# Weights that arrive as 64-bit floats: pieces of 256 columns, a first stage in plain floats, and sign words by two multiplications on GpSimd

## The chip, the core and the metric

One core of one Trainium2 chip runs the kernel. Times are device microseconds of one execution, and fewer is better. The core has five engines, which run side by side: PE (TensorE, the matmuls; its weight loads are listed as PEld), DVE (VectorE), ACT (ScalarE), POOL (GpSimd) and SP, which here only issues DMAs. They wait for each other by semaphores.

## What is computed

```
p_packed = attention(p, k, v)                 # p is [8, 8, 32, 64]; k, v are [8, 8, 576, 64]
out      = attention(q, p_packed, p_packed)   # q is [8, 8, 576, 64]
x = out, heads side by side                   # [4608, 512]
h = x @ w_in                                  # w_in is [512, 2048], float64
g = h * tanh(softplus(h))                     # Mish
result = g @ w_out                            # w_out is [2048, 512], float64; result float32
```

## The kernel before

**The fold.** Since x is the second attention's probabilities times p_packed, the kernel multiplies p_packed into w_in first. For each of the 8 batches it makes a packed weight (`wp`, from `weave`: matmuls `ps_w<-wi,ppT`, ppT being p_packed transposed). Attention then gives only the transposed probabilities `aT`, in two halves g = 0, 1 of 128 rows (4 heads × 32) by 576 tokens. A batch is done in 16 groups, one for each 128 columns of w_in; I count groups as t = 16 b + f.

**A group.** `up(hf)` multiplies the packed weight of 128 columns by `aT` for 288 of the 576 tokens. Each product is made of three matmuls in a faster float format, of values that are split in a high and a low part: `wp_hi, wp_lo` (one cast on ACT, one subtraction on DVE) and `aT_hi, aT_lo` (`upper` and `lower`). So there are six matmuls for each half. ACT applies Mish (`g`). `down(c)` multiplies `g` with 128 rows of w_out into four accumulators `acc`, one group later. In batch 0 the downs multiply plain floats; from batch 1 on they too go in three split passes, for which `split_wo` splits w_out from group 14 on (`wo_hi` on ACT, `wo_lo` on DVE). The last 64 of the 576 tokens are gathered in `g_rest`.

**The weights.** The chip has no 64-bit floats, so each weight is read as two 32-bit words and put together on the chip, in 32 pieces of 512 KB. A piece goes through `fetch` (a DMA on SP's queue into one of STB = 9 stage buffers `w_st`), `words` (two activations on ACT that bring the high word into place and make a rounding word `wround`; on GpSimd a clamp by min and max, and a sign word `wsign` by a multiplication with 0.0), and `join` (on DVE a shift and or, L566, and an add, L570). A w_in piece is 512 columns of one block of 128 rows, so the first four pieces make the packed weight of groups 0 to 3. A w_out piece is 128 rows, for one group. In group t the kernel joins up to piece 2t+7 and starts words up to 2t+9, and a join of n pieces is followed by fetches up to n + STB.

**The opening.** Batch 0's attention runs alone at first, in steps that are written out: `score`, `spread`, `sums`, `values` for p_packed, `match` for the second scores, then for each half `peak` (transposes `a<-ps_s`, a maximum, a subtraction), `rise` (the exponential), `tally` (sum and reciprocal), `divide`, `back` (a transpose to `at`), `upper`, `lower`. `warm(n)` puts n idle matmuls on PE to keep its clock up. Attention of batch 1 is then worked into the groups from t = 4 on (`advance`), with its inputs loaded by `load_next`.

**The order.** PE's order is written by hand all through. SP's, DVE's, ACT's and POOL's are written by hand up to group 16, and left to a scheduler behind it, which may bring instructions forward. Each engine runs its own list in order; what stands at the head of it and waits holds up all behind it.

Of the kernel before, what the change touches and what calls it, by code (L numbers as in the profile page):

```python
# [36 lines left out]
def body(  # L37
# [53 lines left out]
    wi = [[const.tile([P, 2, FC], F32, name=f"wi{c}_{g}") for g in range(2)] for c in range(DF // FC)]  # L91
# [69 lines left out]
    class Batch:  # L161
# [140 lines left out]
        def back(self, g):  # L302
            self.at = att.tile([P, S], F32, name="at", bufs=1)
            nc.vector.transpose(out=self.at, in_=self.a2[:, g].rearrange("a g n -> a (g n)"))

        def upper(self, g):
            nc.scalar.copy(out=self.columns(self.aT_hi[:, g, :]), in_=self.turned_back())  # L307

        def lower(self, g):
            nc.vector.tensor_tensor(  # L310
                out=self.columns(self.aT_lo[:, g, :]), in0=self.turned_back(),
# [3 lines left out]
        def turned_back(self):  # L315
            return self.at.rearrange("a (u x n) -> a u x n", u=2, n=NP) if self.b else self.at
# [25 lines left out]
    class Later(Batch):  # L342
# [39 lines left out]
        def start(self):  # L382
# [3 lines left out]
            self.pp = {}  # L386
# [154 lines left out]
    class Weight:  # L541
# [3 lines left out]
        def __init__(self, c, m):  # L545
            self.c, self.m = c, m

        def fetch(self):
            self.st = stg.tile([P, 2 * FC], I32, name="w_st")
            nc.sync.dma_start(out=self.st, in_=w_in_v[:, self.m, self.c * 2 * FC:(self.c + 1) * 2 * FC])  # L550
            self.dst = wi[self.c][self.m // 2][:, self.m % 2]

        def words(self):
            x = self.st.rearrange("p (n t) -> p n t", t=2)
            self.r = stg.tile([P, FC], I32, name="wround", bufs=WB)
            self.sign = stg.tile([P, FC], F32, name="wsign", bufs=WB)
# [5 lines left out]
            nc.gpsimd.tensor_scalar(out=self.sign, in0=self.dst, scalar1=0.0, scalar2=None, op0=ALU.mult)  # L562

        def join(self):
            dst, bits = self.dst, self.dst.bitcast(I32)
            nc.vector.scalar_tensor_tensor(  # L566
                out=bits, in0=bits, scalar=3, in1=self.sign.bitcast(I32), op0=ALU.logical_shift_left, op1=ALU.bitwise_or
            )
# [12 lines left out]
    def weave(b, c, ps, g, h):  # L581
# [5 lines left out]
            rhs=wi[c][g][row:row + D, h // 2, :],  # L587
# [11 lines left out]
    def packed_half(b, c, g):  # L599
        ps = ps_a.tile([P, FC], F32, name=f"ps_w{g}", tag="ps_a")  # L600
        for h in range(4):
            weave(b, c, ps, g, h)
        return part(ps)

    def packed_w(b, c):

        ps = [ps_a.tile([P, FC], F32, name=f"ps_w{g}", tag="ps_a") for g in range(2)]
        for h in range(4):
            for g in range(2):
                weave(b, c, ps[g], g, h)  # L610
        return [part(x) for x in ps]

# [12 lines left out]
    class Group:  # L625


        def __init__(self, b, f, wp, g_rest):
            self.b, self.f, self.wp, self.g_rest = b, f, wp, g_rest

# [7 lines left out]
        def up(self, hf):  # L638
            aT_hi, aT_lo = batches[self.b].aT_hi, batches[self.b].aT_lo
            fs = slice((self.f % 4) * P, (self.f % 4) * P + P)  # L640
# [3 lines left out]
            for g in range(2):  # L644
                w_hi, w_lo = self.wp[g]
                for w, a in ((w_hi, aT_hi), (w_hi, aT_lo), (w_lo, aT_hi)):
                    nc.tensor.matmul(out=ps, lhsT=w[:, fs], rhs=a[:, g, cs], start=(n == 0), stop=(n == 5))  # L647
                    n += 1
            m = min(HALF, MAIN - hf * HALF)
# [98 lines left out]
    pieces = [Weight(0, m) for m in range(4)]  # L748
    pieces += [WeightOut(0), Weight(1, 0), Weight(1, 1), WeightOut(1), Weight(1, 2), Weight(1, 3)]
    pieces += [WeightOut(2), WeightOut(3)]  # L750
    for c in (2, 3):
        for e in range(2):
            pieces += [Weight(c, 2 * e), Weight(c, 2 * e + 1), WeightOut(4 * c - 4 + 2 * e), WeightOut(4 * c - 3 + 2 * e)]
    pieces += [WeightOut(i) for i in range(12, NF)]
# [18 lines left out]
    with tc.manual_schedule(engines={mybir.EngineType.PE}):  # L773
# [73 lines left out]
        for t in range(n_groups + LAG):  # L847
            b, f = divmod(t, NF)
            grp = None
            if t < n_groups:  # L850
# [87 lines left out]
```

## Time and profile before

| | |
|---|---|
| three runs, us | 769.74, 768.7, 769.67; median 769.67 |
| profiled execution, us | 767.17 |
| its span, first to last instruction, us | 765.4 |
| mean granted clock of PE | 0.992 |
| busy: PE, PEld, DVE, ACT, POOL, us | 737.8, 567.5, 422.9, 296.3, 74.5 |
| first up of group 0, us from the start of the span | 34.16 |

The profile takes one execution apart. A row of its timeline gives the start, the duration, the engine, the line of the kernel, the operation, what it writes and reads, and in brackets how long the engine was idle before it and what released it. A row of its waits gives the engine and line that waited, what for, the total, the number of times and the longest. [...] "PE busy" includes time in which PE runs at a lower clock.

### The profile page before, as it was taken

Reading aid. Unit: us, or ns where it says so; the run is one execution under the profiler, and the core shown is the slowest. Engines: PE = TensorE matmul, PEld = TensorE weight load, DVE = VectorE, ACT = ScalarE, POOL = GpSimd, SP = SyncE. Lnnn points to the kernel's source line nnn. Section 1 sums busy time; section 2 is a strip of 40 time slices with the busy share of each in tenths; the row PEclk is TensorE's granted clock in tenths of the full one; section 3 lists DMA queues with packets and bytes.
Section 4 is the critical chain, followed back from the end, with each engine's and each line's share of the span. In section 5 each row is a group of like instructions: output and inputs, shape, how many; then the busy total and the mean of one; then the engine's idle time right before and its main releaser. Section 6 shows DMA issues by size and latency. Waiting matters only on the chain.

```text
span 765.4 us, 12641 instructions
## 1 busy us (share of the span) xinstructions
PE 737.8 (96%) x5120; PEld 567.5 (74%) x5120; DVE 422.9 (55%) x726; ACT 296.3 (39%) x683; POOL 74.5 (10%) x70
## 2 busy tenths in 40 slices
PE   7788888999999999999999999999999999999997
PEld 6454545577788777877888778878888787888886
DVE  4867758973834647363753737463663647333232
ACT  5455736743422424243333424334332334232221
POOL 2377566000000000000000000000000000000000
PEclk9979999999999999999999999999999999999999
DMA  9999982153301433052401533032300100010002
GB/s 262 330 198 249 205 205 49 27 99 62 64 0 59 81 71 56 1 119 38 93 1 42 97 64 63 1 91 44 77 1 15 56 2 1 1 55 1 1 1 69
DMA packets 184825, 56.39 MB, mean 74 GB/s; under 512 B 173760, under 2 KB 176064, under 8 KB 184768
## 3 DMA queue, kind: packets, MB, share of 16 engines
q1 hardware_dynamic: 184768, 55.59, 31.5%
q8 instruction: 40, 0.66, 0.4%
q14 instruction: 17, 0.14, 0.1%
HBM read 46.14 MB, written 9.44 MB: 73 GB/s over the span
## 4 chain that ended last, share of the span: by engine, by line
PE 84%; POOL 6%; issue 6%; DVE 2%; ACT 1%; POOLq 0%; DVEq 0%; ACTq 0%
PE ps_h L647 24%; PE acc L666 15%; PE acc L668 14%; PE acc L667 14%; POOL wsign L562 4%; PE ps_w L584 4%; PE ps_s L406 3%; PE ps_rest L668 2%; PE ps_rest L667 2%; PE ps_rest L666 2%; PE acc L686 1%; PE ps_pp L461 1%; POOL wo L559 1%; POOL wi L559 1%; PE ps_warm L746 1%
## 5 line engine op out<-in xcount | busy, mean ns | idle before, releaser
L650 ACT ACTIVATE g<-ps_h 128x288 f32<-128x288 f32 (+1 forms) x256 | 97.3, 384 | 324.6 <-PE ps_h L647 294.3
L666 PE MATMUL acc<-wo_hi,g_hi 128*128 128x512 f32 x448 | 183.4, 409 | 0.0
L668 PE MATMUL acc<-wo_hi,g_lo 128*128 128x512 f32 x448 | 176.5, 394 | 0.0
L667 PE MATMUL acc<-wo_lo,g_hi 128*128 128x512 f32 x448 | 176.2, 393 | 0.0
L647 PE MATMUL ps_h<-aT_hi,wp_hi 128*128 128x288 f32 x512 | 166.4, 325 | 2.9 <-ACT aT_hi L307 2.9
L647 PE MATMUL ps_h<-aT_lo,wp_hi 128*128 128x288 f32 x512 | 152.0, 297 | 0.2 <-DVE aT_lo L310 0.2
L647 PE MATMUL ps_h<-aT_hi,wp_lo 128*128 128x288 f32 x512 | 151.4, 296 | 0.0
L661 DVE CAST g_hi<-g 128x512 fp32r<-128x512 f32 x112 | 47.6, 425 | 167.0 <-ACT g L650 166.8
L666 PEld LDWEIGHTS acc<-wo_hi,g_hi 128*128 128x128 f32 x448 | 83.9, 187 | 43.1 <-issue 28.7
L647 PEld LDWEIGHTS ps_h<-aT_hi,wp_hi 128*128 128x128 f32 x512 | 97.2, 190 | 21.7 <-issue 7.5
L647 PEld LDWEIGHTS ps_h<-aT_lo,wp_hi 128*128 128x128 f32 x512 | 97.2, 190 | 17.0 <-issue 7.5
L668 PEld LDWEIGHTS acc<-wo_hi,g_lo 128*128 128x128 f32 x448 | 84.0, 188 | 19.6
L647 PEld LDWEIGHTS ps_h<-aT_hi,wp_lo 128*128 128x128 f32 x512 | 97.1, 190 | 0.2 <-DVE wp_lo L596 0.2
L667 PEld LDWEIGHTS acc<-wo_lo,g_hi 128*128 128x128 f32 x448 | 84.2, 188 | 8.8
L662 DVE TENSOR_TENSOR g_lo<-g,g_hi 128x512 fp32r<-128x512 f32 x112 | 77.3, 690 | 6.4 <-DVE g_hi L661 0.5
L686 PE MATMUL acc<-wo,g 128*128 128x512 f32 x128 | 65.3, 618 | 11.5 <-DVE wo L570 8.3
L596 DVE TENSOR_TENSOR wp_lo<-ps_w,wp_hi 128x512 fp32r<-128x512 f32 x64 | 41.4, 683 | 17.6 <-ACT wp_hi L595 17.6
L595 ACT CAST wp_hi<-ps_w 128x512 fp32r<-128x512 f32 x64 | 34.5, 592 | 35.5 <-PE ps_w L584 35.5
L686 PEld LDWEIGHTS acc<-wo,g 128*128 128x128 f32 x128 | 21.8, 193 | 28.7 <-issue 15.0
L584 PE MATMUL ps_w<-wi,ppT 64*32 64x512 f32 x512 | 38.9, 600 | 0.4 <-DVE wi L570 0.3
L652 ACT ACTIVATE g_rest<-ps_h 128x64 f32<-128x64 f32 x128 | 28.1, 219 | 0.0
L562 POOL TENSOR_SCALAR wsign<-wo 128x512 f32<-128x512 f32 x16 | 27.2, 1702 | 1.3
(109 smaller groups left out, 729.6 us busy)
## 6 DMA issues: line engine op xcount, KB each, us to landing
w_st<-in_moe_w_in_dram SPq DMA_DIRECT2D x16, 512.0 KB, 6.8
w_st<-in_moe_w_out_dram SPq DMA_DIRECT2D x16, 512.0 KB, 6.2
k_n<-in_k_dram SPq DMA_DIRECT2D x56, 144.0 KB, 3.2
q_n<-in_q_dram SPq DMA_DIRECT2D x56, 144.0 KB, 3.2
v_n<-in_v_dram SPq DMA_DIRECT2D x56, 128.0 KB, 2.8
out_dram<-o SPq DMA_DIRECT2D x28, 256.0 KB, 2.0
k_t<-in_k_dram SPq DMA_DIRECT2D x4, 288.0 KB, 3.9
q_t<-in_q_dram SPq DMA_DIRECT2D x4, 288.0 KB, 9.1
```

The lines of the kernel that those rows point to most:

```text
L562: nc.gpsimd.tensor_scalar(out=self.sign, in0=self.dst, scalar1=0.0, scalar2=None, op0=ALU.mult)
L584: nc.tensor.matmul(out=ps[h * NP:(h + 1) * NP, :], lhsT=ppTb[row:row + D, g, h * NP:(h + 1) * NP], rhs=wi[c][g][row:row + D, h // 2, :], s ...
L595: nc.scalar.copy(out=hi, in_=ps)
L596: nc.vector.tensor_tensor(out=lo, in0=ps, in1=hi.bitcast(F32), op=ALU.subtract)
L647: nc.tensor.matmul(out=ps, lhsT=w[:, fs], rhs=a[:, g, cs], start=(n == 0), stop=(n == 5))
L650: nc.scalar.activation(out=self.act[:, hf * HALF:hf * HALF + m], in_=ps[:, :m], func=AF.Mish)
L661: nc.vector.tensor_copy(out=hi, in_=self.act)
L662: nc.vector.tensor_tensor(out=lo, in0=self.act, in1=hi.bitcast(F32), op=ALU.subtract)
L666: nc.tensor.matmul(out=acc, lhsT=hi[:, cs], rhs=wh, start=start, stop=False)
L667: nc.tensor.matmul(out=acc, lhsT=hi[:, cs], rhs=wl, start=False, stop=False)
L668: nc.tensor.matmul(out=acc, lhsT=lo[:, cs], rhs=wh, start=False, stop=stop)
L686: nc.tensor.matmul(out=accs[c], lhsT=grp.act[:, cs], rhs=wo[f], start=f == 0, stop=f == NF - 1)
```

## The change

1. **Pieces of w_in.** A piece is now 256 columns of two blocks of rows, so that two pieces and not four make a packed weight, which then serves two groups and not four. `packed_half(n)` makes it for later groups, in groups 1, 3, ... 13, with casts and subtractions of 256 columns. The list of pieces puts one w_out piece ahead of each pair of w_in pieces and one behind it. The stage has 8 buffers and not 9, `wround` 5 and not 3, `wsign` 3 as before.
2. **Groups 0 and 1 multiply plain floats** (`up_floats`): two matmuls for each half in place of six. The weight for them is only copied out (`packed_first`), and no low parts are needed. Four idle matmuls (`warm_into`) stand between the two g in group 0. `upper` and `lower` move into groups 0 and 1; the half g = 1 is divided and turned back in two steps of 288 tokens, and Mish's table is loaded ahead of group 0.
3. **Sign words.** GpSimd multiplies with 0.0 and then with 1.0, in the same instruction.
4. **Joins.** Group t joins up to piece 2t + 5 (2t + 6 from t = 12 on), and no longer 2t + 7, while words still go up to 2t + 9.
5. **Loads.** `load_next` runs in groups 0, 2, 4, 5 and 6, and batch 2's inputs follow from group 12 on.
6. **Splits of w_out** from the third on stay in the order of the program.

```diff
+    QC = FC // 2                       # FC is 512
-STB = 9
-WB = 3
+STB = 8
+RB = 5
+SB = 3
+LOADS = {0: 1, 2: 1, 4: 1, 5: 1, 6: 1}
+LATER = 12
...
+        if i >= NF - SPLIT0:           # in split_wo
+            for x in both:
+                tc.keep_in_program_order(x)
...
-            nc.gpsimd.tensor_scalar(out=self.sign, in0=self.dst, scalar1=0.0, scalar2=None, op0=ALU.mult)
+                nc.gpsimd.tensor_scalar(
+                    out=self.sign, in0=self.dst, scalar1=0.0, scalar2=SIGN_TWO, op0=ALU.mult,
+                    **({"op1": ALU.mult} if SIGN_TWO else {})
+                )
...
+    def packed_first(g):
+        if g == 0:
+            whole["wp"] = wts.tile([P, 2, QC], F32, name="wp_0", tag="wp_hi", bufs=4)
+        ps = ps_a.tile([P, QC], F32, name=f"ps_w{g}", tag="ps_a")
+        for h in range(4):
+            weave(0, ps, wi[0][g][:, 0, h // 2], g, h)
+        nc.scalar.copy(out=whole["wp"][:, g], in_=ps)
+        return whole["wp"]
...
+        def up_floats(self, hfs, gs):
+            fs = slice(self.f * P, (self.f + 1) * P)
+            for g in gs:
+                for hf in hfs:
+                    if g == 0:
+                        self.ps[hf] = ps_h.tile([P, HALF], F32, name="ps_h", tag="ps_h")
+                    nc.tensor.matmul(
+                        out=self.ps[hf], lhsT=self.wp[:, g, fs],
+                        rhs=batches[0].floats[g][:, hf * HALF:(hf + 1) * HALF], start=(g == 0), stop=(g == 1),
+                    )
+                    if g == 1:
+                        self.mish(hf, self.ps[hf])
...
+    pieces = [Weight(0, 0), Weight(0, 1)]
+    for n in range(1, NF // 2):
+        w = [Weight(n, 0), Weight(n, 1)]
+        pieces += [WeightOut(2 * n - 2)] + w + [WeightOut(2 * n - 1)]
+    pieces += [WeightOut(NF - 2), WeightOut(NF - 1)]
...
-        join(3)
-        words(4)
+        words(3)
         together(first.values(1, ps_a))
         warm(WARM[2])
+        together(first.turn_values(1, ps_a))
         first.tally(slice(0, 1))
-        together(first.turn_values(1, ps_a))
-        first.divide(slice(0, 1))
-        first.back(0)
-        first.upper(0)
         warm(WARM[2])
         together(first.match(1, ps_acc))
         first.peak(slice(1, 2))
-        wps = {(0, 0): []}
         first.rise(slice(1, 2))
-        first.lower(0)
-        join(4)
-        wps[0, 0].append(packed_half(0, 0, 0))
+        first.divide(slice(0, 1))
+        first.back(0)
+        packed_first(0)
+        words(4)
+        wps = {(0, 0): packed_first(1)}
+        nc.scalar.preload_act_table_set("mish")
+        warm(WARM[3])
         first.tally(slice(1, 2))
-        first.divide(slice(1, 2))
-        words(5)
-        warm(WARM[3])
-        wps[0, 0].append(packed_half(0, 0, 1))
-        first.back(1)
-        first.upper(1)
-        first.lower(1)
+        first.back(1, 2)
         words(6)
-        join(5)
...
+            if t == 0:
+                join(3)
             if t <= 13:
-                join(2 * t + 7)
+                join(2 * t + 5 + t // 12)
```

The order of the instructions shows three places. The first is DVE's list at the end of the opening, from the maximum of half g = 1 (`mx_476` before, `mx_460` after) to its transpose back to `at`. Before:

```order
L276 TENSOR_REDUCE mx_476<-a_372 128x18
L277 TENSOR_TENSOR a_372<-a_372,mx_476 128x576
L310 TENSOR_TENSOR aT_lo<-at,aT_hi 128x576
L566 SCALAR_TENSOR_TENSOR wi_1_92<-wi_1_92,wsign 128x512
L570 ISA wi_1_92<-wi_1_92,wround 128x1024
L596 TENSOR_TENSOR wp_lo<-ps_w_485,wp_hi 128x512
L288 TENSOR_REDUCE sm_494<-a_372 128x18
L289 TENSOR_SCALAR sm_494<-sm_494 128x18
L290 RECIPROCAL sm_494<-sm_494 128x18
L294 TENSOR_TENSOR a_372<-a_372,sm_494 128x576
L596 TENSOR_TENSOR wp_lo<-ps_w_517,wp_hi 128x512
L304 STREAM_TRANSPOSE at<-a_372 128x576
```

DVE there after the change, with the join of `wo_228` (w_out's first piece) behind it:

```order
L287 TENSOR_REDUCE mx_460<-a_365 128x18
L288 TENSOR_TENSOR a_365<-a_365,mx_460 128x576
L308 TENSOR_TENSOR a_365<-a_365,sm_441 128x576
L326 STREAM_TRANSPOSE at<-a_365 128x576
L299 TENSOR_REDUCE sm_499<-a_365 128x18
L300 TENSOR_SCALAR sm_499<-sm_499 128x18
L301 RECIPROCAL sm_499<-sm_499 128x18
L308 TENSOR_TENSOR a_365<-a_365,sm_499 128x288
L326 STREAM_TRANSPOSE at<-a_365 128x288
L308 TENSOR_TENSOR a_365<-a_365,sm_499 128x288
L326 STREAM_TRANSPOSE at<-a_365 128x288
L605 SCALAR_TENSOR_TENSOR wo_228<-wo_228,wsign 128x512
```

The join of w_in's fourth piece (`wi_1_92`), both `wp_lo` and `aT_lo` are gone from this stretch, and the division and transpose of half g = 0 have come into it.

The second is PE's list at the start of group 0. Before, from the packed weight's second half (`ps_w_517`) on:

```order
L584 MATMUL ps_w_517<-wi_1_92,ppT 32x512 x4
L647 MATMUL ps_h<-aT_hi,wp_hi 128x288
L647 MATMUL ps_h<-aT_lo,wp_hi 128x288
L647 MATMUL ps_h<-aT_hi,wp_lo 128x288
L647 MATMUL ps_h<-aT_hi,wp_hi 128x288
L647 MATMUL ps_h<-aT_lo,wp_hi 128x288
L647 MATMUL ps_h<-aT_hi,wp_lo 128x288
```

PE there after the change, up to the first down:

```order
L624 MATMUL ps_w_480<-wi_1_92,ppT 32x256 x4
L825 MATMUL ps_warm<-still 128x128 x12
L716 MATMUL ps_h<-at,wp_467 128x288 x2
L829 MATMUL ps_h<-still 128x128 x4
L716 MATMUL ps_h<-at,wp_467 128x288 x2
L761 MATMUL acc_583<-wo_228,g 128x512
```

Four float matmuls, with fillers between the two g, stand for the twelve split ones of group 0 (six of which are shown).

The third is SP's queue of DMAs around the last weight pieces. Before, with loads of p, k and q (`p_n`, `k_n`, `q_n`) for the batches behind between the fetches:

```order
L578 DMA w_st<-in_moe_w_out_dram 128x1024 x2
L377 DMA p_n<-in_p_dram 32x8x32 x4
L351 DMA k_n<-in_k_dram 32x36x32 x4
L550 DMA w_st<-in_moe_w_in_dram 128x1024 x2
L377 DMA p_n<-in_p_dram 32x8x32 x4
L351 DMA k_n<-in_k_dram 32x36x32 x4
L578 DMA w_st<-in_moe_w_out_dram 128x1024 x2
L351 DMA q_n<-in_q_dram 32x36x32 x4
L578 DMA w_st<-in_moe_w_out_dram 128x1024 x4
```

SP there after the change:

```order
L618 DMA w_st<-in_moe_w_out_dram 128x1024 x2
L573 DMA w_st<-in_moe_w_in_dram 128x2x512 x2
L618 DMA w_st<-in_moe_w_out_dram 128x1024 x2
L573 DMA w_st<-in_moe_w_in_dram 128x2x512 x2
L618 DMA w_st<-in_moe_w_out_dram 128x1024 x3
L400 DMA p_n<-in_p_dram 32x8x32 x4
L374 DMA k_n<-in_k_dram 32x36x32 x8
L374 DMA q_n<-in_q_dram 32x36x32 x8
```

All fetches of weights now stand ahead of these loads.

More of the change, by code (lines that the diff above doesn't have):

```diff
@@ L290, in tally, with divide @@
             nc.vector.reciprocal(out=sm, in_=sm)
-        def divide(self, gs):
-            a2 = self.a2[:, gs].rearrange("a h g n -> a (h g) n")
+        def divide(self, gs, half=None):
+            a2, sm = self.a2[:, gs].rearrange("a h g n -> a (h g) n"), self.sm2
+            if half is not None:
+                n = a2.shape[1] // 2
+                a2, sm = (x[:, half * n:(half + 1) * n] for x in (a2, sm))
             nc.vector.tensor_tensor(
-                out=a2, in0=a2, in1=self.sm2.unsqueeze(2).to_broadcast(list(a2.shape)), op=ALU.mult
+                out=a2, in0=a2, in1=sm.unsqueeze(2).to_broadcast(list(a2.shape)), op=ALU.mult
             )
@@ L592, in part @@
     def part(ps):
-        hi = wts.tile([P, FC], F32R, name="wp_hi", bufs=4)
-        lo = wts.tile([P, FC], F32R, name="wp_lo", bufs=4)
+        hi = wts.tile([P, FC], F32R, name="wp_hi", tag="wp_hi", bufs=4)
+        lo = wts.tile([P, FC], F32R, name="wp_lo", tag="wp_lo", bufs=4)
         nc.scalar.copy(out=hi, in_=ps)
@@ L597, in part, with packed_half @@
         return hi, lo
-    def packed_half(b, c, g):
-        ps = ps_a.tile([P, FC], F32, name=f"ps_w{g}", tag="ps_a")
+    def packed_first(g):
+        if g == 0:
+            whole["wp"] = wts.tile([P, 2, QC], F32, name="wp_0", tag="wp_hi", bufs=4)
+        ps = ps_a.tile([P, QC], F32, name=f"ps_w{g}", tag="ps_a")
         for h in range(4):
-            weave(b, c, ps, g, h)
-        return part(ps)
+            weave(0, ps, wi[0][g][:, 0, h // 2], g, h)
+        nc.scalar.copy(out=whole["wp"][:, g], in_=ps)
+        return whole["wp"]
+    def packed_half(n):
+        ps = [ps_a.tile([P, QC], F32, name=f"ps_w{g}", tag="ps_a") for g in range(2)]
+        for h in range(4):
+            for g in range(2):
+                weave(0, ps[g], wi[n // 2][g][:, n % 2, h // 2], g, h)
+        hi = wts.tile([P, 2, QC], F32R, name="wp_hi", tag="wp_hi", bufs=4)
+        lo = wts.tile([P, 2, QC], F32R, name="wp_lo", tag="wp_lo", bufs=4)
+        for g in range(2):
+            nc.scalar.copy(out=hi[:, g], in_=ps[g])
+            nc.vector.tensor_tensor(out=lo[:, g], in0=ps[g], in1=hi[:, g].bitcast(F32), op=ALU.subtract)
+        return [(hi[:, g], lo[:, g]) for g in range(2)]
     def packed_w(b, c):
@@ L746, in warm, with warm_into @@
             nc.tensor.matmul(out=ps_warm, lhsT=still, rhs=still, start=True, stop=True)
[L748 to L754, printed above, removed]
+    def warm_into(ps, n):
+        for _ in range(n):
+            nc.tensor.matmul(out=ps[:, :P], lhsT=still, rhs=still, start=False, stop=False)
+    pieces = [Weight(0, 0), Weight(0, 1)]
[3 more added lines that the diff above has]
+    pieces += [WeightOut(NF - 2), WeightOut(NF - 1)]
     done = {"fetch": 0, "words": 0, "join": 0}
@@ L791, in body @@
         first.score(0)
+        first.turn_keys(1, ("ACT", "DVE", "ACT"))
         first.spread(0)
-        first.turn_keys(1, ("ACT", "DVE", "ACT"))
         first.q_t.append(load_heads(q, 0, 1, "q_t"))
@@ L799, in body @@
         first.score(1)
+        together(first.turn_weights(0, ps_acc, ("DVE", "ACT")))
+        first.spread(1)
         words(2)
-        first.spread(1)
-        together(first.turn_weights(0, ps_acc, ("ACT", "DVE")))
         together(first.turn(0, ps_acc, ("ACT", "DVE", "ACT")))
-        words(3)
         join(1)
@@ L858, in body @@
                     kv.append(ctx.enter_context(tc.tile_pool(name="kv", bufs=2, side="left", reuse_waits="tile")))
-                if t < KQB:
+                owed["t"] = t
+                for _ in range(LOADS.get(t, 0)):
                     load_next()
-                grp = Group(b, f, wps[b, f // 4], g_rest)
+                if t >= LATER and owed["n"]:
+                    owed["n"] -= 1
+                    load_next()
+                grp = Group(b, f, wps[b, f // 4 if b else f // 2], g_rest)
                 grp.tiles()
```

122 lines of the change are left out of this document (85 added, 37 removed).

## The prediction

> **What bounds the kernel now.** I read the stretches of the span first, to find where TensorE is not full.
>
> ```profile
> 0.00:34.20 34.20, 28.27 (x333) 21.91 (x333) 21.74 (x50) 16.52 (x35) 10.48 (x16) 1.00 0.96 307
> 34.20:146.80 112.60, 95.82 (x535) 54.30 (x534) 82.90 (x122) 67.44 (x137) 63.97 (x55) 0.95 0.72 161
> 235.60:320.50 84.90, 84.90 (x617) 67.65 (x616) 47.01 (x82) 29.65 (x70) 0.00 (x0) 1.00 0.30 60
> ```
>
> Columns: stretch, its length, busy time of PE, PEld, DVE, ACT, POOL, granted clock, DMA share, GB/s. 34.2 is the first up matmul of group 0, 146.8 the first of group 16. From 235.6 to 320.5 PE is busy for 84.90 of 84.90 us, and I take the batches behind 146.8 as a fixed tail: a microsecond won or lost before 146.8 reaches the end whole. Ahead of it lie the opening, 16.78 us of idle PE (112.60 − 95.82) and a clock below 1. The waits of PE, and of DVE, in that second stretch:
>
> ```profile
> PE acc L686 <- DVE wo L570: 8.3, 5, 3.5
> PE ps_h L647 <- ACT aT_hi L307: 2.9, 1, 2.9
> PE acc L686 <- ACT wround L558: 2.0, 1, 2.0
> PE ps_ppT L472 <- DVE pp L246: 1.3, 1, 1.3
> PE acc L686 <- ACT g L650: 1.2, 1, 1.2
> PE ps_a L448 <- ACT a L434: 1.0, 1, 1.0
> DVE wo L566 <- POOL wsign L562: 13.2, 8, 4.5
> DVE wi L566 <- POOL wsign L562: 8.6, 7, 2.1
> DVE pT L390 <- DMA p_n<-in_p_dram: 2.8, 1, 2.8
> ```
>
> (Total us, times, longest.) The downs wait for a w_out piece that DVE joins late, and DVE in turn idles 13.2 + 8.6 = 21.8 us for GpSimd's sign words. GpSimd works 63.97 of 112.60 us, so it is late rather than full: a piece is converted at the end of one group and joined in the next.
>
> **The opening (term a).** DVE carries the way to the first whole group. Its rows (start, duration):
>
> ```profile
> 24.06 0.68 DVE L566 SCALAR_TENSOR_TENSOR wi<-wi,wsign 128x512 int32<-128x512 int32 x1
> 25.49 0.35 DVE L246 TENSOR_SCALAR pp<-ps_pp,rs 128x128 f32<-128x128 f32 x1
> 31.05 0.75 DVE L310 TENSOR_TENSOR aT_lo<-at,aT_hi 128x576 fp32r<-128x576 f32 x1
> 31.72 0.68 DVE L566 SCALAR_TENSOR_TENSOR wi<-wi,wsign 128x512 int32<-128x512 int32 x1
> 33.04 0.68 DVE L596 TENSOR_TENSOR wp_lo<-ps_w,wp_hi 128x512 fp32r<-128x512 f32 x1
> 33.64 0.74 DVE L288 TENSOR_REDUCE sm<-a 128x18 f32<-128x576 f32 x1
> 35.61 0.69 DVE L596 TENSOR_TENSOR wp_lo<-ps_w,wp_hi 128x512 fp32r<-128x512 f32 x1
> 36.21 0.77 DVE L304 STREAM_TRANSPOSE at<-a 128x576 f32<-128x576 f32 x1
> 39.53 0.98 DVE L570 CUSTOM_DVE_ANT_0 wo<-wo,wround 128x1024 uint16<-128x1024 uint16 x1
> 37.74 0.61 PE L647 MATMUL ps_h<-aT_hi,wp_hi 128*128 128x288 f32 x1 [2.91 <-ACT aT_hi L307]
> 40.66 2.05 PE L686 MATMUL acc<-wo,g 128*128 128x512 f32 x2
> 29.00 2.94 PE L746 MATMUL ps_warm<-still 128*128 128x128 f32 x24
> ```
>
> From 24.06 to the end of the second transpose back, 36.21 + 0.77 = 36.98, DVE is busy without a gap. The change takes out: the third join (24.06 to 25.49, 1.43), the first aT_lo (31.05 to 31.72, 0.67), the fourth join (31.72 to 33.04, 1.32) and two wp_lo (33.04 to 33.64 and 35.61 to 36.21, 0.60 each): 4.62 us. Those joins are not needed because a first group in pieces of 256 columns needs two pieces and not four; aT_lo and the casts go into groups 0 and 1, and wp_lo is gone since those groups multiply floats. So the transpose would end at 36.98 − 4.62 = 32.4. DVE now has nothing to fill the waits for the PE steps between pp and the scores; I allow 0.9 for them and for the two more instructions of the halves: 33.3. The first half of it is ready about 0.8 earlier, so one up of g = 1 runs ahead of the other.
>
> What is late next is wo_0: its join stands right behind the transpose on DVE. Its two instructions are 0.68 + 0.69 alone and up to 1.1 + 0.98 (the row at 39.53) with GpSimd beside: 33.3 + 1.4 to 2.1 = 34.7 to 35.4, middle 35.1. PE is ready before that: the last float up starts at 33.3. Its price: a float down of 512 columns is two records, and
>
> ```profile
> 142.38 0.80 PE ps_h L647 x6
> 143.18 1.72 PE acc L686 x4
> ```
>
> four records take 1.72, so one down takes 0.86 and a 288-column float matmul 0.86 × 288/512 = 0.48. Two of them per half, 0.97, stand against 0.80 for six split ones: +0.17 per half, +0.34 for group 1, and in group 0 it lies under the wait. The four fillers, a third of the 24 records of 2.94 us, cost 0.98 there, also under the wait for g = 1, and there is no PE idle stretch from the weights' matmuls to the down. ACT loads the Mish table ahead of group 0 and no longer in it. So the first down moves from 40.66 to about 35.1: **−5.5**. The bounds: −6.5 without the 0.9, −4 if the casts on ACT or Mish delay it too.
>
> **The clock (term b).**
>
> ```profile
> 30.00:40.00 10.00, 6.65 (x36) 4.23 (x35) 9.06 (x15) 5.85 (x9) 3.69 (x4) 0.85 0.88 249
> 40.00:50.00 10.00, 7.46 (x24) 4.48 (x22) 6.17 (x8) 6.68 (x16) 9.33 (x9) 0.81 0.94 186
> 50.00:60.00 10.00, 9.00 (x30) 5.52 (x30) 4.36 (x6) 4.10 (x9) 5.61 (x5) 0.83 0.93 232
> 80.00:90.00 10.00, 7.23 (x35) 3.71 (x41) 9.86 (x17) 7.89 (x13) 6.03 (x7) 1.00 0.99 200
> ```
>
> The granted clock is 0.81 and 0.83 in the two stretches behind 40 us. Weighted with PE's busy time that is 7.46 × 0.19 + 9.00 × 0.17 = 2.9 us lost. Each dip follows one long idle stretch (2.91 us before 37.74, and 3.54 before 51.00, below). Both stretches go; a new one may bring back part: **−2** (0 to −2.9). The Trainium skill, "TensorE: Matmul & The Clock Gate", Part 1, says that an idle window of about 3.4 us halves the clock. By that rule only the 3.54 us would count, 9.00 × 0.17 = 1.5 us, and the term would be −1.5; the trace shows 0.81 behind the 2.91 us too, so I count both.
>
> **The join, one group later (term c).** The waits of the downs, one by one:
>
> ```profile
> 51.00 2.04 PE L686 MATMUL acc<-wo,g 128*128 128x512 f32 x2 [3.54 <-DVE wo L570]
> 72.28 1.10 PE L686 MATMUL acc<-wo,g 128*128 128x512 f32 x2 [1.98 <-DVE wo L570]
> 86.85 1.13 PE L686 MATMUL acc<-wo,g 128*128 128x512 f32 x2 [1.81 <-DVE wo L570]
> 117.41 1.10 PE L686 MATMUL acc<-wo,g 128*128 128x512 f32 x2 [1.99 <-ACT wround L558]
> 141.26 1.12 PE L686 MATMUL acc<-wo,g 128*128 128x512 f32 x2 [1.16 <-ACT g L650]
> ```
>
> In group t words are still converted up to piece 2t+9, but joined only up to 2t+5 and not 2t+7. A piece thus has a whole group, 112.60/16 = 7.0 us now, in which GpSimd does two pieces:
>
> ```profile
> 33.68 1.49 POOL wsign L562
> L562 POOL TENSOR_SCALAR wsign<-wo 128x512 f32<-128x512 f32 x16 | 27.2, 1702 | 1.3
> 32.98 0.62 POOL L559 TENSOR_SCALAR wo<-wo 128x512 f32<-128x512 f32 x1 [5.22 <-ACT wo L557]
> ```
>
> Two pieces are 2 × (0.62 + 1.70) = 4.6 us even at the old price of a sign word, which fits. So DVE's 21.8 us of waiting should mostly go, and with them the PE waits at 51.00, 72.28 and 117.41: 3.54 + 1.98 + 1.99 = 7.5. The three sign tiles limit GpSimd to three pieces ahead of DVE; that is still more than a group. In 80 to 90 us DVE is full (9.86 of 10), with batch 1's attention in it; the 1.81 at 86.85, like the 1.0 and 1.3 of the attention's own steps, stays. The 1.16 at 141.26 comes behind a burst of w_out splits on ACT, which program order spreads out: I take half. Together **−8** (bounds: 0 if DVE is late itself, −13.8 for all waits but the one before 37.74).
>
> **The sign word.** One multiplication takes 1.49 alone, 1.70 in the mean; the clamp, which has two operations on the same shape, takes 0.62. The new form has two operations. Nearest row: the clamp, by form; 1.70, by arithmetic. Between them the sum hardly moves, because term c holds at 1.70 already. At 0.62 GpSimd would drop 28 × 1.08 = 30 us, and DVE's instructions beside it would be nearer 0.68 than 1.1. I book 0 and keep that for the range. The Trainium skill, "GPSIMD Engine Reference", 3.1, gives bodies of one and of two operations the same rate. By it the sum stays as it is and rival 2 below falls away; the rows of 1.49 and 0.62 do not agree with it, by form.
>
> **What is new in the way.** Seven chunks of 256 columns stand where three of 512 stood: the columns multiplied are the same, but each chunk ends in two casts and two subtractions with PE's next group right behind, and the join that feeds it is no longer early. Bounds 0 and 1 us each; I take 3 us for all seven, and 0.5 for the starts of the smaller matmuls. Batch 2's p, k, q now stand on SP's queue behind all w fetches:
>
> ```profile
> 73.27 2.05 SPq L377 DMA_DIRECT2D p_n<-in_p_dram  x4
> 79.95 0.45 DVE L390 STREAM_TRANSPOSE pT<-p_n 128x256 f32<-128x256 f32 x1 [2.85 <-DMA p_n<-in_p_dram]
> ```
>
> A p_n issued at 73.27 was used at 79.95, 6.7 us later, after a wait of 2.85 on DVE. The transpose of batch 2's p_n stands on DVE in group 9 ahead of two wp_lo, and its DMA behind the last fetch, which waits for ACT's words at the end of group 8 (two activations, about 1.4 us). Against that DVE has four join instructions of about 0.85 to do, 3.4 us: a stall of 6.7 + 1.4 − 3.4 = 4.7 on DVE. PE needs the wp_lo behind it only in group 10, so most is covered; I book 1 (0 to 4). No other load of batch 2 is wanted before 146.8.
>
> **Sum:** −5.5 − 2 − 8 + 0.3 + 3 + 0.5 + 1 = −10.7. The profiled execution took 767.17 us (span 765.4), and the median of the three runs, 769.67, is 2.5 above: 767.17 − 10.7 = 756.5, as a median **759**.
>
> **Rivals.**
> 1. Only the start moves. The waits re-form since DVE, which loses its idle time but not its 82.90 us of work, becomes late itself at each chunk. For it: 9.86 of 10 in 80 to 90. Against: 82.90 in some 100 us leaves room. Then −5.5 + 1.5 or so: 765.5. Chance 0.18, with the p_n stall as its variant (0.06 more, 764).
> 2. Near the floor. The sign word falls to 0.62, DVE's instructions get shorter, and the new waits do not show: −5.5 − 2.9 − 11 (of the 13.8) + 0.8 = −18.6, 751. Chance 0.19.
> 3. Slower: the second multiplication costs as much as the first, 3.4 in place of 1.70. Then 28 pieces take 28 × (0.62 + 3.4) = 113 us, as long as the whole stretch of 112.60; w_out's last pieces arrive as late as now and every down waits for GpSimd, with DVE's instructions at 1.1 throughout. That is some 0 to 6 us slower, 773; it decides from 112.60/28 − 0.62 = 3.4 us for a sign word. Against: the clamp's two operations in 0.62. Chance 0.06.
> 4. No change, since start and new chunk waits cancel: 0.03.
>
> Forecast as summed: 0.48. A difference under 0.2%, 1.5 us, is about what these runs cannot tell from none. Faster gets 0.48 + 0.24 + 0.19 less some tail of rival 1: 0.88; same 0.05; slower 0.07. The range goes from the floor's 751 to 766, rival 1's time.
>
> **What would show it.** Right: the first down at 34.7 to 35.4; no DVE wait of over 2 us for a sign word; a granted clock near 1 from 40 to 60; group 16 starting near 136; behind it the batches as long as now (84.9 for 235.6 to 320.5). Wrong: PE waits on wp_lo or on the chunk's wi in groups 3 to 13 that sum to more than 5 us, a DVE wait for p_n in group 9 that reaches PE, or sign words over 3 us.

## The result, and the profile after

| | before | changed |
|---|---|---|
| runs, us | 769.74, 768.7, 769.67, 767.46 | 762.2, 762.14, 759.43, 759.7 |
| median, us | 769.18 | 760.92 |
| profiled execution, us; span, us | 767.17; 765.4 | 762.2; 760.1 |

The changed kernel is faster: ratio 0.9896, interval 0.9871 to 0.9921, or 8 us. The forecast was 759 with a range of 751 to 766. A second set of the same kernel (e5 below) gave a ratio of 0.9881 (0.9857 to 0.9905).

The stretches of the span up to the first down, from there to the first up of group 16, and the rest. First before (first down at 40.66, group 16 at 146.85), then changed:

```profile
0.00:40.66 40.66, 31.63 (x345) 24.56 (x345) 27.17 (x58) 20.72 (x42) 13.69 (x18) 0.96 0.95 288
40.66:146.85 106.19, 92.50 (x524) 51.68 (x523) 77.52 (x114) 63.29 (x131) 60.76 (x53) 0.97 0.71 160
146.85:765.40 618.55, 613.67 (x4256) 491.21 (x4254) 318.26 (x556) 212.26 (x512) 0.00 (x0) 1.00 0.21 45
```

```profile
0.00:38.35 38.35, 32.12 (x349) 25.84 (x349) 21.98 (x53) 19.35 (x42) 7.79 (x17) 0.91 0.97 274
38.35:139.39 101.04, 93.28 (x582) 51.57 (x583) 79.91 (x118) 59.48 (x130) 44.00 (x54) 0.98 0.73 180
139.39:760.10 620.71, 614.37 (x4256) 491.15 (x4254) 323.54 (x565) 217.17 (x521) 0.00 (x0) 1.00 0.21 45
```

The same three of e5, the changed kernel in a second profiled execution of 758.27 us:

```profile
0.00:34.76 34.76, 29.23 (x348) 23.96 (x349) 22.13 (x53) 19.35 (x42) 8.00 (x17) 1.00 0.96 274
34.76:135.99 101.23, 93.36 (x582) 51.22 (x583) 80.46 (x118) 59.68 (x130) 44.24 (x54) 0.98 0.76 189
135.99:756.10 620.11, 614.20 (x4256) 491.15 (x4254) 323.24 (x565) 217.15 (x521) 0.00 (x0) 1.00 0.21 45
```

| part of the span, us | forecast | first profile | e5 |
|---|---|---|---|
| to the first down | −5.5 | −2.3 | −5.9 |
| first down to group 16 | −5.2 | −5.2 | −5.0 |
| the rest | 0 | +2.2 | +1.6 |
| sum | −10.7 | −5.3 | −9.3 |

The middle holds idle PE of 106.19 − 92.50 = 13.7 us before, and 7.8 and 7.9 in the two profiles after. The waits of PE after, from 28 to 142 us, and the two rows of DVE's joins, whose last part is DVE's idle time ahead of them:

```profile
PE ps_w L624 <- DVE a L449: 1.9, 1, 1.9
PE acc L761 <- DVE wo L610: 1.6, 1, 1.6
PE ps_pp L484 <- DVE wp_lo L657: 1.6, 1, 1.6
PE acc L761 <- ACT g L725: 1.5, 2, 1.1
PE acc L761 <- ACT g_rest L727: 1.4, 1, 1.4
PE ps_h L706 <- DVE wp_lo L657: 1.0, 1, 1.0
...
L605 DVE SCALAR_TENSOR_TENSOR wi<-wi,wsign 128x512 int32<-128x512 int32 x16 | 12.0, 782 | 0.5 <-POOL wsign L590 0.5
L605 DVE SCALAR_TENSOR_TENSOR wo<-wo,wsign 128x512 int32<-128x512 int32 x16 | 11.9, 778 | 0.0
```

DVE idled 21.8 us for sign words before and 0.5 now, and the joins cost PE 1.6 us in place of 8.3.

### The profile page after: what moved, and what is told of

It reads as the page before. It is cut to its first block, busy times and chain, and to the rows that moved or that the text cites. A ratio compares the mean times of both kernels' runs of the same rounds, so it can differ in the third digit from the quotient of the medians.

```text
span 760.1 us, 12781 instructions
## 1 busy us (share of the span) xinstructions
PE 739.8 (97%) x5184; PEld 568.6 (75%) x5184; DVE 425.4 (56%) x734; ACT 296.0 (39%) x691; POOL 51.8 (7%) x70
## 4 chain that ended last, share of the span: by engine, by line
PE 84%; DMA 4%; DVE 4%; ACT 4%; SPq 1%; issue 1%; DVEq 0%; ACTq 0%
PE ps_h L706 24%; PE acc L741 15%; PE acc L743 13%; PE acc L742 13%; PE ps_w L624 4%; PE acc L761 3%; PE ps_s L429 2%; DMA q_t<-in_q_dram 2%; PE ps_rest L743 2%; PE ps_rest L742 2%; PE ps_rest L741 2%; PE ps_pp L484 2%; DMA out_dram<-o 1%; PE ps_a L471 1%; DMA q_n<-in_q_dram 1%
## 5 line engine op out<-in xcount | busy, mean ns | idle before, releaser
L706 PE MATMUL ps_h<-aT_hi,wp_hi 128*128 128x288 f32 x504 | 162.2, 322 | 0.3 <-ACT g L725 0.3
L706 PE MATMUL ps_h<-aT_hi,wp_lo 128*128 128x288 f32 x504 | 148.5, 295 | 1.0 <-DVE wp_lo L657 1.0
L706 PE MATMUL ps_h<-aT_lo,wp_hi 128*128 128x288 f32 x504 | 148.7, 295 | 0.0
L706 PEld LDWEIGHTS ps_h<-aT_hi,wp_hi 128*128 128x128 f32 x504 | 94.9, 188 | 17.2 <-issue 4.5
L706 PEld LDWEIGHTS ps_h<-aT_lo,wp_hi 128*128 128x128 f32 x504 | 95.0, 189 | 15.9 <-issue 6.7
L706 PEld LDWEIGHTS ps_h<-aT_hi,wp_lo 128*128 128x128 f32 x504 | 94.8, 188 | 1.2 <-DVE wp_lo L657 1.2
L636 DVE TENSOR_TENSOR wp_lo<-ps_w,wp_hi 128x512 fp32r<-128x512 f32 x56 | 36.1, 683 | 17.5 <-ACT wp_hi L635 17.5
L635 ACT CAST wp_hi<-ps_w 128x512 fp32r<-128x512 f32 x56 | 30.1, 590 | 32.8 <-PE ps_w L624 32.8
L624 PE MATMUL ps_w<-wi,ppT 64*32 64x512 f32 (+1 forms) x576 | 38.6, 556 | 3.2 <-DVE a L449 3.2
L761 PEld LDWEIGHTS acc<-wo,g 128*128 128x128 f32 x128 | 21.4, 192 | 22.4 <-issue 11.8
L742 PE MATMUL ps_rest<-wo_lo,r_hi 128*128 128x512 f32 x64 | 25.1, 392 | 0.0
```

The source lines that it names most:

```text
L624: nc.tensor.matmul(out=ps[h * NP:(h + 1) * NP, :], lhsT=ppTb[row:row + D, g, h * NP:(h + 1) * NP], rhs=w[row:row + D], start=True, stop=Tr ...
L635: nc.scalar.copy(out=hi, in_=ps)
L636: nc.vector.tensor_tensor(out=lo, in0=ps, in1=hi.bitcast(F32), op=ALU.subtract)
L742: nc.tensor.matmul(out=acc, lhsT=hi[:, cs], rhs=wl, start=False, stop=False)
L761: nc.tensor.matmul(out=accs[c], lhsT=grp.act[:, cs], rhs=wo[f], start=f == 0, stop=f == NF - 1)
```

## The experiments

All are timed beside the kernel before, with 4 to 12 runs each; e1 to e4 ran together, then e5 to e8 on another chip, then e9 to e12 on the first again; "on the same chip" below means out of one such four.

| | median, us | ratio to before | interval |
|---|---|---|---|
| e1 one multiplication | 764.37 | 0.9949 | 0.9929 to 0.9970 |
| e2 before, two multiplications | 763.77 | 0.9941 | 0.9921 to 0.9961 |
| e3 joins early | 776.73 | 1.0108 | 1.0090 to 1.0127 |
| e4 split ups | 762.95 | 0.9935 | 0.9912 to 0.9958 |
| e5 changed kernel again | 760.04 | 0.9881 | 0.9857 to 0.9905 |
| e6 splits free | 767.89 | 0.9972 | 0.9948 to 0.9996 |
| e7 pT in order | 758.33 | 0.9864 | 0.9842 to 0.9885 |
| e8 q_t first | 764.67 | 0.9944 | 0.9925 to 0.9963 |
| e9 loads as before | 759.41 | 0.9875 | 0.9845 to 0.9905 |
| e10 e7 and 3 fillers | 758.67 | 0.9867 | 0.9842 to 0.9893 |
| e11 e7 and a later join | 755.89 | 0.9849 | 0.9820 to 0.9878 |
| e12 e7 and both | 757.41 | 0.9857 | 0.9831 to 0.9883 |

**e1 and e2, the price of the sign word.** Edits:

```diff
-SIGN_TWO = 1.0      # e1, in the changed kernel
+SIGN_TWO = None
-    scalar1=0.0, scalar2=None, op0=ALU.mult                  # e2, in the kernel before
+    scalar1=0.0, scalar2=1.0, op0=ALU.mult, op1=ALU.mult
```

> The changed kernel with the sign word by one multiplication again (scalar2 None); all else as changed. Theory slack: the extra group between words and join covers GpSimd at its old price, so the time stays within 1.5 us of the changed kernel's 760.9, DVE waits under 4 us for sign words in all, and group 16 still starts near 139 to 141. Theory price: the cheaper sign word is what took DVE's waits away, so DVE waits 10 us or more for sign words and the time is 765 or more.

> The kernel before with one edit: the sign word by two multiplications. Joins, pieces and opening are those of before. Theory slack: DVE still joins a piece one group after its words; the sign word falls from 1.70 to 0.62, and about a third of the PE waits for joins goes: 766 to 769. Theory price: the waits of DVE for GpSimd (21.8 us) and the PE waits for joins (8.3 us) go: 762 or less.

A sign word by two multiplications takes 0.62 alone and 0.94 with DVE beside it, as the changed kernel's timeline shows:

```profile
33.88 0.62 POOL L590 TENSOR_SCALAR wsign<-wi 128x512 f32<-128x512 f32 x1
...
38.75 0.94 POOL L590 TENSOR_SCALAR wsign<-wo 128x512 f32<-128x512 f32 x1
```

The price is worth about 4 us in either kernel: e1 loses 0.0053 to 0.0068 of the ratio, 4 to 5 us, and e2 gains 0.0059, 4.5 us. Neither theory as stated covers that. In e2 DVE still waits 16.0 of the 21.8 us for sign words:

```profile
DVE wo L568 <- POOL wsign L562: 9.3, 8, 4.2
...
DVE wi L568 <- POOL wsign L562: 6.7, 5, 2.4
```

So in the old order most of that wait is the place of the join and not GpSimd's speed. PE's wait for the joins falls from 8.3 to 3.7 us there, while one for an attention step on ACT rises from 1.0 to 4.6. In e1 DVE's wait stays at 2.0 us, as theory slack has it, and yet PE loses. From the first down to group 16 the profile of e1 takes 3.5 us more than that of e5, 2.0 of them idle PE and 1.5 busy PE:

```profile
35.08:139.84 104.76, 94.91 (x582) 52.31 (x583) 78.84 (x118) 59.63 (x130) 63.38 (x55) 0.97 0.73 182
```

The place of the idle time is group 9. DVE and PE there in e1, then in e5:

```profile
87.08 1.09 DVE L605 SCALAR_TENSOR_TENSOR wo<-wo,wsign 128x512 int32<-128x512 int32 x1
93.20 0.45 DVE L413 STREAM_TRANSPOSE pT<-p_n 128x256 f32<-128x256 f32 x1 [5.03 <-DMA p_n<-in_p_dram]
...
95.81 1.45 PE L484 MATMUL ps_pp<-v_n,a1T_n 128*32 128x64 f32 x40 [3.60 <-DVE wp_lo L657]
```

```profile
88.45 2.11 DVE L610 CUSTOM_DVE_ANT_0 wo<-wo,wround 128x1024 uint16<-128x1024 uint16 x2
92.81 0.45 DVE L413 STREAM_TRANSPOSE pT<-p_n 128x256 f32<-128x256 f32 x1 [2.25 <-DMA p_n<-in_p_dram]
...
93.62 0.90 PE L484 MATMUL ps_pp<-v_n,a1T_n 128*32 128x64 f32 x40 [1.66 <-DVE wp_lo L657]
```

In e1, where only the form of the sign word differs, the scheduler puts pT between the two joins of the group instead of behind them. The joins, and wp_lo behind them, then wait for the p_n that is late in both kernels, and PE waits 3.60 in place of 1.66. No run has the dear sign word with pT in its other place, so that pT's place is what PE pays for is read from these rows and not tested by itself. Both openings are alike there (first down 35.08 and 34.76).

**e3, the extra group.**

```diff
-                join(2 * t + 5 + t // 12)
+                join(2 * t + 7)
```

> The changed kernel with joins up to piece 2t+7 in each group again, so that a piece is joined one group after its words and not two; sign words by two multiplications. Theory slack: DVE waits again for sign words, 5 us or more in all, and the downs for joins; 763 to 766. Theory price: at 0.62 to 0.94 us a sign word GpSimd is done in time anyway; within 1.5 us of 760.9.

It is slower than the kernel before, by 16 us against the changed kernel, with the cheap sign words. Its waits:

```profile
PE ps_h L706 <- DVE wp_lo L657: 4.1, 1, 4.1
PE ps_w L624 <- DVE a L449: 3.7, 1, 3.7
PE ps_pp L484 <- DVE wp_lo L657: 3.7, 1, 3.7
...
DVE wo L605 <- POOL wsign L590: 12.7, 7, 4.2
DVE wi L605 <- POOL wsign L590: 9.2, 5, 4.8
```

DVE waits 21.9 us (from 28 us on) for sign words of 0.72 us in the mean, since ACT starts the words at the end of the group before. PE does not wait for those pieces: it waits for wp_lo and attention steps that stand behind the join in DVE's list. The first of these waits, 4.1 us, has little to do with sign words: DVE is idle for only 0.52 us from 36.66 to its end at 52.83, and two joins more than in the changed kernel stand ahead of that wp_lo. From the first down to group 16 e3 takes 115.88 us, 14.7 more than e5, of which 7.8 are idle PE and 6.9 busy PE at a mean clock of 0.93. Without the slack nothing of the change is left; what the slack is worth in the order of before, no run shows.

**e4, the plain floats.** Edits: `packed_half(0)` for `packed_first`, `upper` and `lower` back in the opening, `up` in place of `up_floats`:

```diff
-        packed_first(0)
+        first.upper(0)
+        first.lower(0)
         words(4)
-        wps = {(0, 0): packed_first(1)}
+        wps = {(0, 0): packed_half(0)}
...
         first.back(1, 2)
+        first.upper(1)
+        first.lower(1)
```

> The changed kernel with the plain-float ups of groups 0 and 1 undone: six split matmuls for each half, the packed weight of the first chunk split in high and low, and the casts and subtractions of aT back in the opening. Pieces of 256 columns, loads, joins and sign words as changed. If the float ups shorten the way to the first down as the prediction says, the two wp_lo of 256 columns (0.8), the first aT_lo (0.7) and the second aT cast and subtraction (1.4) come back on that way: the first down 2.5 to 3 us later and the time 762.5 to 764. If the late q_t alone bounds the opening and DVE has room behind it: within 1 us of 760.9.

```profile
31.56 0.61 PE L706 MATMUL ps_h<-aT_hi,wp_hi 128*128 128x288 f32 x1 [2.86 <-ACT wp_hi L656]
36.08 0.61 PE L706 MATMUL ps_h<-aT_hi,wp_hi 128*128 128x288 f32 x1 [3.43 <-ACT aT_hi L329]
```

PE waits for the casts as expected, 2.86 and 3.43 us, and a stretch at half clock (0.50 granted) goes with it, 0.90 in the mean up to the first down. The first down is at 39.00, 4.2 us behind that of e5, where 2.5 to 3 were expected; neither profile has a wait for q_t. The median is 2 us and the ratio 0.0039 to 0.0054 behind the changed kernel, 3 to 4 us, so the float ups pay about that.

**e5, the same kernel again.**

> The changed kernel once more, unedited, beside the next three on one chip. Its runs differ by 2.7 us (759.43 to 762.2), and its profile has a first down at 38.35 where the run with one multiplication had 35.08 with the same opening. If the opening's length varies with when q_t lands and where the half clock falls, then this profile shows another first down, between 35 and 38.5; if 38.35 is the kernel's own, it is there again within 0.3.

The first theory holds, though 34.76 lies a little below its 35. The step that differs is the second q_t on PE, in the first profile and in e5, with the first down of each:

```profile
20.96 0.35 PE L154 MATMUL ps_kq<-ident,q_t 96*128 96x96 f32 x2 [0.82 <-DMA q_t<-in_q_dram]
22.00 1.44 PE L154 MATMUL ps_kq<-ident,q_t 96*128 96x96 f32 x10 [0.68 <-DMA q_t<-in_q_dram]
...
38.35 1.10 PE L761 MATMUL acc<-wo,g 128*128 128x512 f32 x2 [1.38 <-ACT g_rest L727]
```

```profile
21.16 1.22 PE L154 MATMUL ps_kq<-ident,q_t 96*128 96x96 f32 x12 [0.24 <-ACT a1T L146]
...
34.76 1.10 PE L761 MATMUL acc<-wo,g 128*128 128x512 f32 x2 [1.32 <-ACT g_rest L727]
```

Where q_t comes late, PE idles 0.82 and 0.68 us, and its clock is down in the next stretches (0.75 and 0.57, below); in e5 it is 1.00 throughout the opening. The two first downs lie 3.6 us apart, of the 3.9 between the two executions. Most of the 3.6 is the clock: up to the first down PE is busy for 32.12 us against 29.23, 2.9 more, and idle for only 0.7 more. The changed kernel's runs, 758.27 to 763.98 in e5, spread by 5.7.

**e6, the splits of w_out.** The three lines with `keep_in_program_order` in `split_wo` are taken out.

> The changed kernel without the program order for the splits of w_out: ACT's list again has the wo_hi casts in one burst around group 15. The prediction gave half of the 1.16 us wait to the program order. If the order is worth that or more: 0.5 to 3 us slower, with PE waiting for g or wp behind the burst at the end of batch 0. If the wait only changes its place, as the 1.13 us at 138.83 suggests: within 0.5 us.

It is 7 us slower than e5 on the same chip (0.0091 of the ratio), more than either theory gave it. ACT, PE and DVE of e6 around group 15:

```profile
141.11 0.62 ACT L113 CAST wo_hi<-wo 128x512 fp32r<-128x512 f32 x1 [0.58 <-DVE wo_lo L114]
143.67 0.72 ACT L326 CAST aT_hi<-at 128x576 fp32r<-128x576 f32 x1 [1.94 <-DVE at L323]
...
144.67 2.07 PE L758 MATMUL acc<-wo,g 128*128 128x512 f32 x2 [6.29 <-ACT g L722]
```

```profile
133.73 2.48 DVE L114 TENSOR_TENSOR wo_lo<-wo,wo_hi 128x512 fp32r<-128x512 f32 x4
...
139.26 1.82 DVE L114 TENSOR_TENSOR wo_lo<-wo,wo_hi 128x512 fp32r<-128x512 f32 x3
```

Left free, the wo_lo come between the steps of batch 1's `tally`, `divide` and `back` on DVE. ACT's next Mish stands behind aT_hi, which waits for `back`, and PE waits 6.29 us for that Mish. The opening of this profile is a late one (first down at 39.51), ahead of any split; from there to group 16 it takes 9.3 us more than e5, 5.6 of them idle PE. The program order does not remove the old wait (1.16 before, 1.11 in e5); it keeps a larger one from arising in the new order.

**e7, the p_n behind the last fetch.**

```diff
-            nc.vector.transpose(
+            x = nc.vector.transpose(
                 out=self.pT.rearrange("a g n -> a (g n)"), ...
             )
+            if self.b == 2:
+                tc.keep_in_program_order(x)
```

> The changed kernel with batch 2's pT transpose kept in program order, behind group 16, and not in group 9, where it waits for a p_n that is issued behind the last weight fetch (2.1 to 5.0 us in the traces so far). If that wait delays wp_lo and through it PE (1.6 to 3.6 us at ps_pp): no DVE wait for p_n, no PE wait of over 0.5 us at ps_pp, 1 to 3 us faster. If PE would wait there for something else anyway: within 1 us.

The wait for p_n and the one at ps_pp are both gone from its profile, where e5 has 2.25 and 1.66. The median is 1.7 us below e5's on the same chip; the intervals of the ratios (0.9842 to 0.9885, and 0.9857 to 0.9905) overlap, so the times alone do not settle its worth. The stretch from the first down to group 16 says more:

```profile
34.37:133.83 99.46, 93.24 (x583) 51.49 (x583) 79.57 (x117) 59.63 (x130) 44.03 (x54) 0.98 0.77 192
```

It takes 99.46 us against 101.23 in e5 and 101.04 in the first profile, and 99.42 in e10, which has the same edit. So the late p_n costs about 1.7 us there, nearly all of it idle PE (6.2 us against 7.9 in e5).

**e8, q_t ahead of w_in's second piece.** The line `fetch(2)` ahead of `first.start(ps_a)` is taken out, so that the piece follows with `fetch(STB)` behind q_t.

> The changed kernel with w_in's second piece fetched behind the second q_t and not ahead of it. If the q_t that shares the DMA engines with weights bounds the opening: PE waits for q_t under 0.3 us, the first down at 35 or earlier in the profile, 1 to 3 us faster in the median. If the opening is bound elsewhere, or the weight piece then comes late: within 1 us, or slower with a PE wait for wi.

```profile
22.97 1.21 PE L163 MATMUL ps_s<-qT,ppT 64*32 64x288 f32 x16 [4.19 <-ACT qT L146]
...
DVE wi L605 <- POOL wsign L590: 4.6, 1, 4.6
```

It is 4.6 us slower. The weight piece is now the late one: its words stand ahead of qT's copies in ACT's list, and PE waits 4.19 us for qT, DVE 4.6 for the sign word. Putting q_t first only changes which load comes late.

**e9, the loads.** `LOADS = {0: 1, 1: 1, 2: 1, 3: 1, 4: 1}` and `LATER = 0`, as before.

> The changed kernel with the loads as before: one in each of groups 0 to 4, and batch 2's p, k and q between the last weight fetches. If putting the weights first on SP's queue helps, as the diff arranges it: weight pieces land later, words and joins follow, and it is 2 us or more slower. If weights have room by then (GpSimd waits for ACT and not for DMAs in this stretch): within 1.5 us of the changed kernel, or up to 2 us faster, since p_n is no longer behind the last fetch.

No difference that these runs can tell from none (0.9875). The order of the loads is not what makes the change faster. Its profile says that the new order of the loads rather costs: with the loads as before, the wait for p_n and the one at ps_pp are gone as in e7, and the stretch from the first down to group 16 is as short as there.

```profile
38.21:137.52 99.31, 94.66 (x583) 51.81 (x583) 80.24 (x118) 59.70 (x130) 43.93 (x54) 0.97 0.79 189
```

That is 1.9 us less than in e5, with one profile of each; the opening of e9's was a late one (38.21).

**e10 to e12, three fillers and a join.** `warm(3)` ahead of the second `first.turn(1, ...)` (e10, e12), and in e11 and e12:

```diff
-                join(2 * t + 5 + t // 12)
+                join(2 * t + 5 + t // 12 - (t == 1))
```

> e7 (pT in order) with three more idle matmuls on PE ahead of the second q_t transposes. In the profiles with a late q_t, PE idles 1.5 us there and runs at half clock from 22.5 to 29.3, and the first down comes 3.6 us later than in those without. If idle PE causes that: no half clock in the opening and a spread of the runs under 2 us, median 0.5 to 1.5 us faster than e7's ratio of 0.9864. If q_t's landing alone delays it, the same or up to 0.7 us slower.

> e7 with one join moved: group 1 joins wo_1 alone, and wo_2, which group 3 needs, is joined in group 2. In groups 0 to 2 DVE is full (19.7 of 20 us from 30 to 50), and PE waits 1.64 us for wo_1 and 0.98 for wp_lo. If DVE's list there is what PE waits for: both waits go, 1.5 to 2.6 us faster than e7's ratio of 0.9864. If the 2.1 us only come up again in group 2 or 3, ahead of the next chunk: within 0.7 us of it.

> e7 with the three idle matmuls and the moved join. If e10 and e11 each gain, the sum of both: a ratio of 0.982 to 0.984. If one gains alone, that one's.

The fillers change nothing that can be measured (0.9867 against 0.9864). Neither profile with them has a half clock in the opening, but e7's has none without them. Leaving e4 and e8 aside, whose edits delay the opening themselves, the late openings (first profile, e3, e6, e9 and e11, with first downs from 38.21 to 40.04) all have a half clock of 6.8 us that begins between 21.4 and 23.1 us, behind waits for q_t, v_t or qT; the early ones (e1, e5, e7, e10 and e12, 34.37 to 35.41) have none. Yet e2, in the order of before, idles 1.16 and 0.83 us for q_t at the same place and keeps its full clock. So a late opening and a half clock go together in the new order, and what sets off the half clock stays open. In e11 PE's two waits in group 2 of e7, 1.64 and 0.98, become one of 0.63, and the chunk after that waits 2.95 in place of 1.95:

```profile
47.21 1.10 PE L763 MATMUL acc<-wo,g 128*128 128x512 f32 x2 [0.63 <-DVE wo L612]
...
69.83 1.52 PE L626 MATMUL ps_w<-wi,ppT 64*32 64x256 f32 x16 [2.95 <-DVE a L451]
```

That is a gain of 1 us net, and its median of 755.89 is the lowest of all. It beats both kernels' medians; against e7 its interval decides nothing. Nor does e12's: its profile has 1.0 us less idle PE in the middle than e10's, but a half clock of 6.8 us in place of one of 3.4, which takes that back.

## Why the prediction came out right, and where it did not

**The sum.** The direction came out, and so did the middle of the span (−5.2 forecast, −5.2 and −5.0 measured); the whole came to 8.3 us between the medians, and 9.7 in e5, of the 10.7 forecast. But the middle agrees by terms that missed on both sides. Its idle PE fell by 5.9 us where −4 was booked, and PE's busy time, which the clock, the float ups and the smaller matmuls together were to lower by 1.2 us, rose by 0.8 (92.50 to 93.28). That the two cancel is luck. Nor are the parts of the change shares of a sum: taking back the slack, the order of the splits, the float ups or the cheap sign word costs about 16, 7, 4 and 4 us, some 30 in all, of a change of 8, so each has that worth only beside the others. What the pieces of 256 columns are worth by themselves, no run shows.

**The opening.** The DVE chain was worked out well: back(1) was forecast to end at 33.3 and wo_0 to be joined by 34.7 to 35.4; in e5 they end at 32.6 and 34.6, and the first down is at 34.76. What the prediction left out is that DVE is not the only engine on that way. PE takes up the second q_t ahead of values and scores; in the first profile (38.35) it waits 1.5 us for that DMA and runs at half clock behind it, so only 2.3 of the 5.5 us show. The row for it was there before the change, with a wait too short to stand out:

```profile
22.50 1.04 PE L143 MATMUL ps_kq<-ident,q_t 96*128 96x96 f32 x10 [0.20 <-DMA q_t<-in_q_dram]
```

The term's bound of −4 should have been −2. The clock, in the seventh column, in stretches of the first profile:

```profile
20.00:25.00 5.00, 3.50 (x63) 2.81 (x62) 2.56 (x6) 3.08 (x8) 0.00 (x0) 0.75 1.02 362
25.00:30.00 5.00, 5.00 (x48) 3.70 (x49) 2.57 (x7) 0.65 (x2) 1.23 (x2) 0.57 1.03 386
...
40.00:50.00 10.00, 7.37 (x38) 3.69 (x37) 10.00 (x13) 6.71 (x16) 8.40 (x10) 1.00 0.96 256
50.00:60.00 10.00, 10.00 (x54) 5.72 (x53) 8.15 (x13) 5.80 (x15) 4.75 (x6) 1.00 0.96 224
70.00:75.00 5.00, 5.00 (x25) 3.06 (x13) 3.16 (x6) 1.97 (x6) 0.22 (x1) 0.66 0.96 289
```

**The clock.** From 40 to 60 it is 1.00, as forecast, but in the first profile the half clock has moved to the opening, behind idle pieces of under 1 us each, and to 70 us, behind the wait of 1.95 at a chunk. In e5 the same wait of 1.95 leaves the clock at 1.00 (66 to 71), and a half clock follows the wait of 1.66 at 93.62 (0.66 from 95 to 100). So the length of one wait does not decide it. By the prediction's own weighing, 2.9 us came back from 40 to 60 and 5.00 × 0.34 = 1.7 were lost again in either profile: −1.2 in place of −2. The rule of the Trainium skill that the prediction weighed ("TensorE: Matmul & The Clock Gate", Part 1) asks for an idle window; these rows show the clock down after windows that were only partly idle.

**The joins, one group later.** Right in kind: DVE's 21.8 us went, and without the slack (e3) they are back. The −8 for PE measured as −5.9 of idle time with the new chunk waits in it, against −4 for term and new waits together. The waits that I took for stayers did not stay: the 1.81 at 86.85 and the 1.0 and 1.3 of the attention's own steps are gone. Others came, all of them for DVE: 1.64 and 0.99 at the first chunk, where DVE is full from 40 to 50 (10.00 of 10), 1.95 for an attention step at 69, and 1.55 behind the late p_n.

**The sign word.** Booked at 0; e1 and e2 put it at about 4 us. The step that failed is "the sum hardly moves, because term c holds at 1.70 already": DVE no longer waits for GpSimd, true, but with a dear sign word the scheduler also puts pT elsewhere. The price by form (0.62) was the right end; the Trainium skill's equal rate for one and two operations ("GPSIMD Engine Reference", 3.1) does not agree with 1.49 for one and 0.62 for two on the same 512 elements.

**The p_n behind the last fetch.** Forecast as a stall of 4.7 us on DVE with 1 us of it on PE; DVE's stall was 2.1 to 5.0, and PE's wait at ps_pp 1.6 to 3.7 in the runs of the new order that have it. The mechanism was right and its price on PE too low.

**The splits.** Booked at half of 1.16; e6 puts the order at 7 us. I read its worth from the wait of before, which it hardly changes, and did not ask what the free burst does in the new lists.

**The fixed tail.** Before, PE was full behind 146.8, so I took it as fixed. It gave back 2.2 us (618.55 to 620.71). Two waits after group 16 are new, of 1.2 us together, and the later one is released by a DVE list that a late o copy holds up:

```profile
PE ps_w L624 <- DVE a L449: 1.2, 2, 0.9
...
324.82 0.69 DVE L750 COPY o<-acc 128x512 f32<-128x512 f32 x1 [1.58 <-DMA out_dram<-o]
```

A third, of 0.3 us, is for ACT's g. The other 0.7 us is busy PE (613.67 to 614.37) and was not traced further.

## What to carry to other kernels

When an engine waits for a helper, look first at where the waiting instruction stands in its list: what stands behind it is what PE pays for, and here moving the join back one group did more (16 us) than a helper twice as fast (4). A full engine behind the change is no proof of a fixed tail, and a chain on one engine only gives the gain down to the next transfer that the other engines wait for. Where a scheduler fills in the order, every changed price moves other instructions too, so compare lists and not only durations.

## What the runs showed of the hardware

A second multiplication made GpSimd's instruction faster: 1.49 us with one operation, 0.62 with two, on the same 128x512 floats. With the short form GpSimd and DVE slow each other about evenly: 0.93 to 0.94 for GpSimd's two instructions and 1.0 to 1.1 for each instruction of DVE's joins, against 0.62 and 0.7 alone. The half clock took stretches of 3.4 or 6.8 us in most profiles (70.3 to 73.7 and 22.5 to 29.3 in the first), and one of 10.2 in e4. It fell at other places in two executions of one kernel, and makes up 2.9 of the 3.6 us between their first downs.
